# First query block of a fused attention and GEGLU kernel: four key segments, one scheduled step at a time, loads in two waves, output sums preloaded before the last PV

## Chip, cores, metric

The kernel runs on one core of a Trainium2 chip. The metric is the device time of one execution in microseconds (us), and quoted medians are over the executions of a run. All inputs and the output are bf16.

A run is called *fast* or *slow* by its own group: an execution over 1.5% above the fastest of the same kernel is slow.

## The reference, cut to what matters

```python
xn = layernorm(x)                                   # x: 2048 x 448
q, k, v = split(xn @ wqkv)                          # 16 heads of 28
a = softmax(q @ k.T * 28**-0.5) @ v                 # 16 heads, 2048 x 2048 scores
h = gelu_tanh(xn @ w_gate) * (xn @ w_up)            # 448 -> 1792
out = x + concat(a) @ wo + h @ w_down
```

## The kernel before

The kernel is one static program for five engines. Its order is fixed by a scheduler that runs on the host while the program is built. The scores make 1024 units (query block of 512, head group of 4 heads, key tile of 128, head). Three units form a *slot*: three score matmuls into one PSUM tile `st` of 128x1536, then one exp on ScalarE. The exps `e` are later multiplied with v into the tile `ot`; these matmuls are called *PV*. There are 342 slots. Everything else has to fit between the slots, as *steps* of about four matmuls and one copy out of PSUM: transposes of the normalized input, projections of q, k and v, the MLP, the output products, the softmax normalization. All steps share one PSUM buffer (`aux`, one bank), so a step can start on TensorE only after DVE has copied the step before it out.

The first query block is special, because k and v do not exist yet. It runs in two key segments. The first four key tiles of all four head groups come first, then key tiles 4 to 15 of each head group in turn:

```python
SEG = 4
blocks = [(0, hg, 0, SEG) for hg in range(NHG)] + [(0, hg, SEG, NKC) for hg in range(NHG)]
blocks += [(Q, hg, 0, NKC) for Q in range(1, NQ) for hg in range(NHG)]
```

Steps with a deadline (a slot number) stand in `todo`, where `due(Q, hg, kc)` is the slot that first needs key tile `kc` of head group `hg` for query block `Q`; the MLP, the output products and later q projections stand in `lazy`:

```python
for T in range(1, NQ):                      # 512 rows of keys each
    for t0 in (4 * T, 4 * T + 2):
        add(due(0, 0, 4 * T) - 6, 1, lambda t0=t0: g_transpose(t0))
    for hg in range(NHG):
        add(due(0, hg, 4 * T) - 4.5, 1, lambda hg=hg, T=T: g_proj(1, hg, T))
for tt in range(NT):
    add(due(0, 0, tt) + 0.5 if tt >= SEG else 2 + tt, 1, lambda tt=tt: g_v(tt))

def run_slot():
    if cur[0] is None:                      # else: the MLP or output product in hand goes on
        if urgent:                          #       to its last step (up to four slots)
            cur[0] = urgent.pop(0)()
        elif todo and (todo[0][0] <= now[0] + 2 or not lazy):
            cur[0] = todo.pop(0)[2]()
        elif lazy:
            ...
```

In the main loop, a step that has become late is forced into the present slot, and so is the next one. Other steps wait for `credit`, which grows by the steps left over the slots left; a step costs one. `backlog` is the scheduler's estimate of TensorE work still queued, in ns:

```python
if overdue or aux_open[0] or ((credit[0] >= 1.0 or p >= END) and backlog + C_SLOT <= dt + 600):
    ev = run_slot()
    ...                                     # credit -= 1
    while todo and todo[0][0] < p - 0.6:    # still late: a second, a third step in this slot
        ...
        ev = run_slot()
        credit[0] -= 1.0
if not ev and not aux_open[0]:              # no step: dummy matmuls, to keep the clock up
    nj = int((0.85 * dt - backlog) / 216)
    if nj > 0:
        jp = aux.tile([P, QT], F32, tag="a", name="jp")
        junk(jp[:], nj)
        backlog += 216 * nj
```

At the start, the whole q and k weight (784 KB) is loaded before the first head group can be padded into place. At the end, the four output sums so far (`pre`, as a high and a low bf16 part) are put into PSUM by eight identity matmuls behind the last PV:

```python
preload(0)
while len(pv_q) > 4: emit_pv(pv_q.pop(0))
preload(1); preload(2)
while pv_q: emit_pv(pv_q.pop(0))
fb = spool.tile(...); fins[3] = fb[:, 0:D]
preload(3)
otb = ...; nc.scalar.copy(otb[:], ot_cur[0][:])
junk(fa[:, 2 * QT :], 1)
...                                         # sums, reciprocal, product `on`, last output matmuls
```

The softmax here doesn't subtract the row's maximum and nothing guards it: scores larger than these inputs give would overflow.

## Time and profile before

| before | us | from |
|---|---|---|
| median | 565.5 (3 runs, 563.6 to 569.5) | first times |
| profiled execution | span 563.5, clock 0.962 | cores view |
| first exp starts / last exp ends | 15.6 / 552.5 | ScalarE timeline |
| after the last exp | 11.0 | the same |
| 342 exps, 28 tanhs in an unbroken row | about 482 | pitches 1.335 and 0.945 us, estimate |
| idle ScalarE between first and last exp | 55.3 | see below |

The page first: its span, engine totals, and two rows of 40 slices (14.1 us each). Digits are tenths of busy time; PEclk is the granted clock of TensorE in tenths.

```profile
span 563.5 us, 8188 instructions
...
PE 482.1 (86%) x3228; PEld 155.0 (28%) x3253; DVE 256.5 (46%) x491; ACT 501.5 (89%) x383; POOL 13.2 (2%) x44
...
ACT  4679779878669999999998999999999999999993
...
PEclk9699998997679999999999999999999999999999
```

ScalarE (ACT) is the busiest engine, and after slice 13 it is near 9 throughout. Before that it is not, and some low digits stand above a low clock. A table of windows makes two stretches of it: busy time per engine, instruction counts in brackets, then the granted clock.

```profile
core 0: us, PE busy (x) PEld busy (x) DVE busy (x) ACT busy (x) POOL busy (x), PEclk, DMA share, GB/s
0.00:80.00 80.00, 63.87 (x411) 23.22 (x413) 46.13 (x123) 58.31 (x48) 13.18 (x44) 0.94 0.32 75
80.00:190.00 110.00, 91.03 (x552) 26.46 (x558) 46.05 (x80) 89.38 (x67) 0.00 (x0) 0.86 0.10 26
```

Between 80 and 190 us ScalarE is busy for 89.4 of 110 us. For finer numbers I took each exp's and tanh's start in the trace, less the start before it and its pitch (1.335 us after an exp, 0.945 after a tanh); what is left is idle ScalarE. By slot it is 15.1 us in slots 0 to 39, **23.0 us in slots 40 to 99**, and 17.2 us in the 242 slots after. These three numbers are used for every run below; each comes from the one profiled execution of that kernel.

One stall inside, from the timeline (start, duration, engine, line, operation, output from inputs; in brackets how long the engine sat idle before it, and what released it):

```profile
121.02 0.69 DVE L376 TENSOR_TENSOR gu<-gups,g 128x512 bf16<-128x512 f32 x1 [1.19 <-PE gups L326]
121.76 0.38 PE L398 MATMUL bt<-rr_175,sel 128*128 128x512 bf16 x1 [0.78 <-DVE gu L376]
...
122.18 0.69 DVE L401 TENSOR_TENSOR on<-otsb,bt 128x512 bf16<-128x512 f32 x1 [0.47 <-PE bt L398]
122.92 1.02 PE L281 MATMUL pp<-xnT_199,wqk_sb 112*128 112x512 bf16 x4 [0.78 <-DVE on L401]
...
123.98 0.69 DVE L288 CAST kT_3_1428<-pp 128x512 bf16<-128x512 f32 x1 [1.11 <-PE pp L281]
...
124.73 1.02 PE L494 MATMUL st<-qT,kT_3_1428 28*128 28x512 bf16 x6 [0.79 <-DVE kT_3_1428 L288]
...
125.43 1.45 ACT L508 ACTIVATE e<-st 128x1536 bf16<-128x1536 f32 x1 [3.73 <-PE st L494]
```

Three steps (an MLP step, a normalization, a key projection; this is slot 61) pass through the one `aux` buffer one after another, TensorE and DVE taking turns; the scores need the projected key, and ScalarE waits 3.7 us. The window of 3.41 us around it is the last before the clock was halved, and so with another at 87 us (TensorE alone; columns: window, its length, busy time, granted clock):

```profile
87.23:90.65 3.42, 1.38 (x17) 1.00 0.04 7
121.37:124.78 3.41, 1.45 (x9) 1.00 0.23 67
```

The half-clock stretches are 19.0 to 29.2, 90.7 to 94.1, 124.8 to 135.0 and 145.3 to 162.3 us, 41 us together. Last, the tail (timeline; the exps are merged, x2):

```profile
550.44 2.02 ACT L508 ACTIVATE e<-st 128x1536 bf16<-128x1536 f32 x2
...
553.14 0.40 PE L521 MATMUL ot<-e,va_163 128*32 128x512 bf16 x4
553.62 0.59 ACT L786 CAST otb<-ot 128x512 bf16<-128x512 f32 x1 [1.16 <-PE ot L521]
...
554.35 0.35 PE L773 MATMUL f_5956<-prehi,ident 128*128 128x448 bf16 x1
...
555.67 0.35 PE L773 MATMUL fb<-prelo,ident 128*128 128x448 bf16 x1
...
556.07 0.24 PE L789 MATMUL fb<-selc,otb 128*128 128x4 bf16 x4
...
557.63 0.69 DVE L811 TENSOR_TENSOR on<-otb,fb 128x512 bf16<-128x512 bf16 x1 [0.56 <-PE fb L802]
...
560.69 0.35 ACTq L825 DMA_DIRECT2D out_dram<-res  x1
```

The copy `otb` is done at 554.2, but the sums that read it start at 556.07, because the preloads stand in between.

### The profile page before, as it was taken

The numbers are of one execution on the slowest core, as the hardware profiler recorded it, in microseconds if no ns is written. First come the engines' busy times: TensorE is split into PE (matmuls) and PEld (weight loads), VectorE is DVE, ScalarE is ACT, GpSimd is POOL, SyncE is SP. The second block draws the span as 40 slices with busy tenths as digits, with TensorE's granted clock in tenths as the row PEclk, the third lists the DMA queues.
The fourth block names the chain that finished last, engine by engine and source line by source line (L and its number), as shares of the span: only waits on it lengthen the run. The fifth ranks groups of instructions, "written<-read, shape, count | busy, mean of one in ns | idle before, by whom it ended". The sixth has DMA issues, their size and how long they took to land.

```text
span 563.5 us, 8188 instructions
## 1 busy us (share of the span) xinstructions
PE 482.1 (86%) x3228; PEld 155.0 (28%) x3253; DVE 256.5 (46%) x491; ACT 501.5 (89%) x383; POOL 13.2 (2%) x44
## 2 busy tenths in 40 slices
PE   7878788878788888988988899888888898989986
PEld 3223332222222222322222332222222232223322
DVE  5668332443345541155655312666646512671241
ACT  4679779878669999999998999999999999999993
POOL 4310000000000000000000000000000000000000
PEclk9699998997679999999999999999999999999999
DMA  9800000110111100021211002031101101200000
GB/s 212 202 11 1 2 0 2 31 36 1 34 33 28 42 1 18 16 68 33 67 34 34 1 18 58 26 84 49 51 17 34 35 18 49 66 2 0 3 1 33
DMA packets 39685, 20.43 MB, mean 36 GB/s; under 512 B 7328, under 2 KB 39648, under 8 KB 39648
## 3 DMA queue, kind: packets, MB, share of 16 engines
q1 hardware_dynamic: 38560, 18.83, 12.8%
q10 hardware_dynamic: 1088, 1.09, 0.7%
q8 instruction: 25, 0.41, 0.3%
q14 instruction: 12, 0.10, 0.1%
HBM read 17.89 MB, written 1.84 MB: 35 GB/s over the span
## 4 chain that ended last, share of the span: by engine, by line
PE 54%; DVE 18%; ACT 17%; issue 8%; DMA 2%; POOL 0%; ACTq 0%; POOLq 0%; DVEq 0%
PE gups L326 18%; ACT e L508 16%; PE st L494 9%; PE ot L521 9%; PE jp L549 5%; PE op L418 5%; DVE gu L376 4%; PE pp L281 4%; DVE g L337 4%; PE pv L295 3%; DMA wst<-in_A_wqkv_dram 2%; ACT th L357 1%; DVE qT L288 1%; DVE zz L352 1%; DVE on L401 1%
## 5 line engine op out<-in xcount | busy, mean ns | idle before, releaser
L508 ACT ACTIVATE e<-st 128x1536 bf16<-128x1536 f32 x342 | 470.9, 1467 | 44.5 <-PE st L494 38.0
L337 DVE CAST g<-gups 128x512 bf16<-128x512 f32 x56 | 38.7, 691 | 65.6 <-PE gups L326 65.6
L549 PE MATMUL jp<-zt 128*128 128x512 bf16 x124 | 42.9, 396 | 18.5 <-DVE g L337 4.8
L376 DVE TENSOR_TENSOR gu<-gups,g 128x512 bf16<-128x512 f32 x56 | 38.7, 691 | 43.9 <-PE gups L326 43.9
L418 PE MATMUL op<-wd_sb,ht 128*128 128x448 bf16 x224 | 50.7, 354 | 0.8 <-DVE qT L288 0.5
L326 PEld LDWEIGHTS <-wu 112*128 112x128 bf16 x224 | 19.1, 98 | 41.3 <-issue 27.9
L357 ACT ACTIVATE th<-zz 128x1024 bf16<-128x1024 bf16 x28 | 29.9, 1069 | 0.0
L326 PEld LDWEIGHTS <-wg 112*128 112x128 bf16 x224 | 19.0, 98 | 39.3 <-issue 26.6
L549 PEld LDWEIGHTS <-zt 128*128 128x128 bf16 x182 | 16.8, 101 | 36.8 <-issue 28.7
L418 PEld LDWEIGHTS <-ht 128*128 128x128 bf16 x224 | 18.2, 98 | 27.0 <-issue 15.3
L352 DVE TENSOR_TENSOR zz<-po,g 128x1024 bf16<-128x1024 bf16 x28 | 19.2, 687 | 0.5
L368 DVE TENSOR_TENSOR ht<-ph,gu 128x1024 bf16<-128x1024 bf16 x28 | 19.2, 686 | 0.4
L342 DVE TENSOR_TENSOR sq<-g 128x1024 bf16<-128x1024 bf16 x28 | 19.2, 686 | 0.3
L281 PEld LDWEIGHTS <-wqk_sb 112*128 112x128 bf16 x128 | 11.3, 101 | 26.5 <-issue 17.6
L326 PE MATMUL gups<-xnT_199,wu 112*128 112x512 bf16 x56 | 14.4, 379 | 3.7 <-DVE g L337 2.8
L288 DVE CAST qT<-pp 128x512 bf16<-128x512 f32 x15 | 10.4, 691 | 15.4 <-PE pp L281 15.4
L326 PE MATMUL gups<-xnT_199,wg 112*128 112x512 bf16 x56 | 14.4, 380 | 2.5 <-DVE gu L376 1.4
L326 PE MATMUL gups<-xnT_197,wu 112*128 112x512 bf16 x56 | 14.5, 380 | 2.3 <-DVE gu L376 1.8
L326 PE MATMUL gups<-xnT_198,wu 112*128 112x512 bf16 x56 | 14.5, 380 | 2.3 <-DVE g L337 1.4
L326 PE MATMUL gups<-xnT_198,wg 112*128 112x512 bf16 x56 | 14.4, 380 | 2.3 <-DVE g L337 1.8
L326 PE MATMUL gups<-xnT_197,wg 112*128 112x512 bf16 x56 | 14.5, 381 | 1.4 <-DVE g L337 1.4
L418 PE MATMUL op<-wo_sb,on 128*128 128x448 bf16 x60 | 14.1, 354 | 1.3 <-DVE pre L464 1.0
(263 smaller groups left out, 606.4 us busy)
## 6 DMA issues: line engine op xcount, KB each, us to landing
wg<-in_B_w_gate_dram SPq DMA_DIRECT2D x28, 224.0 KB
wu<-in_B_w_up_dram SPq DMA_DIRECT2D x28, 224.0 KB
wd_sb<-in_B_w_down_dram SPq DMA_DIRECT2D x1, 1568.0 KB
out_dram<-res SPq DMA_DIRECT2D x14, 112.0 KB
den<-otsb SPq DMA_DIRECT2D x60, 2.0 KB
rr_174<-recb SPq DMA_DIRECT2D x32, 1.0 KB
x_119<-in_A_x_dram SPq DMA_DIRECT2D x1, 448.0 KB
x_120<-in_A_x_dram SPq DMA_DIRECT2D x1, 448.0 KB
```

Of the source, the lines that this page charges most:

```text
L281: nc.tensor.matmul(pp[:, 0:QT] if ps is None else pp, lhsT=wqk_sb[:, comp, hg, c, :], rhs=xnc(T, c), start=(c == 0), stop=(c == NDC - 1),)
L326: nc.tensor.matmul(ps[:], lhsT=w[:, c, k * P : (k + 1) * P], rhs=xnc(Q, c), start=(c == 0), stop=(c == NDC - 1),)
L337: yield ("evac", C_EVAC, lambda ps=ps, k=k: nc.vector.tensor_copy(g[:, k, :], ps[:]))
L342: nc.vector.tensor_mul(st["a"][:], g[:], g[:])
L352: nc.vector.tensor_mul(st["z"][:], st["b"][:], g[:])
L357: nc.scalar.activation(st["t"][:], st["z"][:], AF.Tanh, scale=TANH_SCALE)
L376: yield ("evac", C_EVAC, lambda ps=ps, k=k: nc.vector.tensor_mul(gu[:, k, :], ps[:], g[:, k, :]))
L418: nc.tensor.matmul(ps[:, 0:D], lhsT=l, rhs=r, start=(first and n == 0), stop=(last and n == len(seq) - 1))
L494: nc.tensor.matmul(st[:, j * QT : (j + 1) * QT], lhsT=kT[(hg, kc // 4)][32 * hh : 32 * hh + Dh, (kc % 4) * P : (kc % 4 + 1) * P], rhs=qT[( ...
L508: nc.scalar.activation(e[:, 0:n], st[:, 0:n], AF.Exp, scale=SCALE)
L521: nc.tensor.matmul(ot_cur[0][32 * hh : 32 * hh + 32, :], lhsT=vaug[kc][:, h * 32 : (h + 1) * 32], rhs=e[:, j * QT : (j + 1) * QT], start=( ...
L549: nc.tensor.matmul(ps, lhsT=zt[:, 0:P], rhs=zt[:], start=True, stop=True)
```

## The change

The intent: spread what the first query block needs, so that no pile forms; start earlier; end earlier.

```diff
-    blocks = [(0, hg, 0, SEG) for hg in range(NHG)] + [(0, hg, SEG, NKC) for hg in range(NHG)]
+    blocks = [(0, hg, k, k + SEG) for k in range(0, NKC, SEG) for hg in range(NHG)]
@@ closing a block: one accumulator per head group, added to in place
@@ layer norm in four groups (statistics from slot 0, 12, 30 on), not two
@@ deadlines
-            add(due(0, 0, 4 * T) - 6, 1, lambda t0=t0: g_transpose(t0))
-            add(due(0, hg, 4 * T) - 4.5, 1, lambda hg=hg, T=T: g_proj(1, hg, T))
-        add(due(0, 0, tt) + 0.5 if tt >= SEG else 2 + tt, 1, lambda tt=tt: g_v(tt))
+            add(first - 6 + k, ln_p0[T] + 10 + 2 * k, lambda t0=4 * T + 2 * k: g_transpose(t0))
+            add(due(0, hg, 4 * T) - 4, ln_p0[T] + 13, lambda hg=hg, T=T: g_proj(1, hg, T))
+            add(first - 2 + 1.4 * k, ln_p0[T] + 13, lambda tt=4 * T + k: g_v(tt))
@@ slot rule: the MLP may be interrupted after each step; eight slots of look-ahead
+        if todo and todo[0][0] <= p + 1:
+            return step(todo.pop(0)[2]())
+        if urgent:
+            return step(urgent.pop(0)())
+        if todo and todo[0][0] <= p + LOOK and todo[0][1] <= p:
+            return step(todo.pop(0)[2]())
+        ...                                   # due q projections, then the MLP in hand, then lazy
-        overdue = bool(urgent) or (todo and todo[0][0] <= p) or (lazy and any(...))
+        overdue = (todo and todo[0][0] <= p) or any(...)
@@ fewer dummies
-            nj = int((0.85 * dt - backlog) / 216)
+            nj = int((0.75 * dt - backlog) / 216) if p < NP - 2 else 0
@@ first wave of loads: x rows 0-511 and the weights of head group 0 alone (196 KB)
+    nc.sync.dma_start(wst0[:, :, 0, :], wv_ap[:, :, 0 : 4 * Dh])
+    nc.scalar.dma_start(wst0[:, :, 1, :], wv_ap[:, :, D : D + 4 * Dh])
+    ...                                       # the rest once these have landed
@@ tail
-    fins = [f0[:, 0:D], fa[:, 0:D], fa[:, QT : QT + D], None]
+    fins = [f0[:, 0:D]] + [fa[:, k * QT : k * QT + D] for k in range(3)]
+    for tl in range(TPQ):
+        preload(tl)
     while pv_q:
         emit_pv(pv_q.pop(0))
-    junk(fa[:, 2 * QT :], 1)                  # and two more places
+    junk(fb[:, 0:QT], 1)
```

No exp, tanh, projection or output product is added or removed. Eight more blocks are closed.

## The prediction

> **What bounds the kernel now.** ScalarE: the page has it busy 89% of 563.5 us. In the timeline, exps in an unbroken row come 1.335 us apart (the last 18 span 23.65 us); a tanh takes about 0.945 us of the row. 342 exps and 28 tanhs need about 482 us (estimate from those pitches). The span is 15.6 us before the first exp, 537 between first and last (482 of work, 55 idle), 11.0 after the last.
>
> Counting exps in slices of the ScalarE timeline, about 38 us of the idle fall before 190 us (81 exps have started by 160 us; an unbroken row would allow 108), 17 us in the 362 us after. The first query block needs all keys and values between slots 21 and 37, then 9 more key projections just ahead of use; its MLP, which could fill TensorE, starts near 100 us. The waits name scores (`st`) and `ot`. At 121-125 us a just-in-time chain shows: bt, DVE, pp, DVE, scores; ScalarE idles 3.7 us. After such gaps the table of windows shows a granted clock of 0.50: about 19-29, 91-94, 125-135 and 145-162 us, 41 us in all; four projection matmuls there take 1.9 us, not 1.0. The Trainium skill, "TensorE: Matmul & The Clock Gate", Part 1, says that an idle TensorE is gated to half clock until busy for a window; the trace agrees.
>
> **What the change does.**
> 1. Four key segments: deadlines fall at slots 21, 42 and 64, and the MLP fills between. No exp, tanh or projection is removed. Added: 8 block closings (0.69 us DVE each; `ot` has one buffer, so TensorE waits up to 0.8 us each); perhaps 2-4 us of it shows.
> 2. One step at a time by deadline, looking 8 slots ahead: fewer chains, fewer cold clocks. The MLP starts early, so later phases thin out.
> 3. Small first load: the chain now waits for the 785 KB `wst`, landing at 10.3 us. The first wave is 200 KB, so pads move to about 8.4 us, after the exp table load; transposes end near 10.1. First exp at about 14 us: gain 1.5-2.
> 4. Tail: 8 preloads (1.5 us) and junk stand between the last exp (552.5) and the sums (556.1). Gain about 2 us; last exp to end about 9.
> 5. Less junk (0.75 for 0.85): some risk of a cold clock.
>
> **Critical path.** Items 1 and 2 hit ScalarE's idle before 190 us. Estimate: 38 falls to about 12 there, 17 to about 14 after. 14 + 482 + 26 + 9 = 531 us span; the measured time was 2 above the span, so **533 us**, range **522 to 547**. Faster by over 2%: 0.94; within 2%: 0.05; slower: 0.01.
>
> **What would show each step.** Right: first exp at 13.5-14.5 us; about 100 exps and tanhs by 160 us; tanhs from about 25-35 us on; clock row near 9 except perhaps one dip in the first 30 us, under 15 us cold; about 9 us after the last exp; counts and pitches unchanged. Wrong: cold stretches of 10 us past 40 us; ScalarE waiting for `st` in slots 21-85; `ot` waits of 1 us at each closing.
>
> **What would make it wrong.** The pile moves to segment boundaries, where transposes, projections and values still chain over one auxiliary PSUM buffer and DVE; MLP weights land late behind the second wave; less junk lets the clock drop in steady state; the MLP competes and the steady 17 us grow. Upside: even load takes steady idle below 10 us: about 522.

## The result and the profile after

The median fell from 564.5 us (4 runs, 558.3 to 569.5) to 536.4 us (4 runs, 536.4 to 538.2). The ratio of the fast runs is 0.9545, with a 95% interval from 0.946 to 0.963. A ratio is the mean time of one kernel's fast runs over that of the other's in the same rounds, so it is not quite the ratio of the quoted medians. The profiled executions took 565.7 us (before, slow) and 538.2 us (after, fast, the slowest of its four); the mean of the fast runs before is 562.4 us, so about 3 us of the difference between the two profiles belong to the slower state.

The same rows of the page after (a slice is now 13.4 us):

```profile
span 536.4 us, 8127 instructions
...
PE 460.5 (86%) x3174; PEld 152.1 (28%) x3194; DVE 265.8 (50%) x514; ACT 498.5 (93%) x382; POOL 18.4 (3%) x71
...
ACT  4777899999999999999999999999999999999993
...
PEclk9686999999999999999999999999999999999999
```

The table of windows:

```profile
0.00:80.00 80.00, 67.09 (x407) 22.90 (x409) 45.36 (x128) 59.85 (x48) 17.80 (x68) 0.85 0.29 78
80.00:190.00 110.00, 93.40 (x669) 30.61 (x671) 63.95 (x115) 107.75 (x83) 0.62 (x4) 1.00 0.10 27
```

Between 80 and 190 us ScalarE is now busy for 107.8 of 110 us. Before 80 us almost nothing has changed: 59.9 us against 58.3, and the clock there is even lower than before.

The whole 27.1 us of span between the two profiled executions can be added up: the first exp comes 1.75 us earlier (13.82 for 15.57), ScalarE's idle falls by 25.0 us (55.3 to 30.3), and the time after the last exp by 0.35 us (11.05 to 10.7). By slot the idle fell by 0.8 us in slots 0 to 39 (to 14.3), by **20.9 us in slots 40 to 99 (to 2.1)** and by 3.3 us after (to 13.9).

Three windows of 3.41 us ahead of the clock drops that remain (TensorE alone):

```profile
13.41:16.82 3.41, 2.07 (x16) 1.00 1.16 304
33.89:37.30 3.41, 1.44 (x18) 1.00 0.00 0
47.54:50.95 3.41, 1.94 (x16) 1.00 0.00 0
```

The clock was halved right after each: 16.8 to 27.1, 37.3 to 47.5 and 51.0 to 54.4 us, 24 us together for 41 before. The middle one in the timeline:

```profile
33.74 0.40 PE L500 MATMUL st<-qT,kT_0_505 28*128 28x512 bf16 x4 [0.46 <-DVE qT L294]
35.71 0.39 PE L500 MATMUL st<-qT,kT_0_505 28*128 28x512 bf16 x3 [1.57 <-ACT e L514]
...
37.39 1.03 PE L287 MATMUL pp<-xnT_201,wqk_sb 112*128 112x512 bf16 x2
```

By its matmul records TensorE waits 1.57 us for an exp, in slots where the scheduler placed no step and a single dummy, because its backlog count said that TensorE was late. That dummy is missing among the matmuls: the program places 88 dummies in the loop, all weight loads are in the trace (this one at 34.06 us), but only 70 of the matmuls. In e6, with the same loop and all 88 records, the window at this place (34.55 to 37.96 us) is busy for 1.76 us with no gap over 1.25 us, and the clock was halved after it too. Two projection matmuls then take 1.03 us; at full clock two took 0.60 (at 15.64 us).

The first tanh comes late, on ScalarE's timeline:

```profile
94.74 1.20 ACT L363 ACTIVATE th<-zz 128x1024 bf16<-128x1024 bf16 x1
```

It was at 114 us before; the MLP still does not fill the first 80 us. The tail:

```profile
523.54 2.17 ACT L514 ACTIVATE e<-st 128x1536 bf16<-128x1536 f32 x2
...
525.31 0.36 PE L777 MATMUL f_5930<-prehi,ident 128*128 128x448 bf16 x1
...
526.93 0.40 PE L527 MATMUL ot<-e,va_159 128*32 128x512 bf16 x4
...
528.05 0.25 PE L788 MATMUL fb<-selc,otb 128*128 128x4 bf16 x4 [0.72 <-ACT otb L785]
...
530.05 0.69 DVE L810 TENSOR_TENSOR on<-otb,fb 128x512 bf16<-128x512 bf16 x1 [0.99 <-PE fb L552]
...
531.76 0.53 ACT L823 CAST res<-fa 128x448 bf16<-128x448 f32 x1 [3.77 <-PE fa L812]
...
532.33 0.62 DVE L823 CAST res<-fa 128x448 bf16<-128x448 f32 x1 [0.51 <-ACT res L823]
532.99 0.53 ACT L823 CAST res<-fa 128x448 bf16<-128x448 f32 x1 [0.69 <-DVE res L823]
```

From the end of the last exp to the sums is 2.3 us (525.71 to 528.05), against 3.6 before (552.46 to 556.07): 1.3 us gained. But the last PV now waits behind the eight preloads (526.93, although its exp ended at 525.71), `on` waits for dummies in its own tile `fb` (0.99 us idle for 0.56 before), and the copies on ScalarE and DVE take turns on tile `fa`, where before one of them read `fb` at the same time. Most of the 1.3 us is given back.

### The profile page after: what moved, and what is told of

Read it like the earlier page. It is cut to its first block, busy times and chain, and to the rows that moved or that the text cites. A ratio compares the mean times of both kernels' runs of the same rounds, so it can differ in the third digit from the quotient of the medians.

```text
span 536.4 us, 8127 instructions
## 1 busy us (share of the span) xinstructions
PE 460.5 (86%) x3174; PEld 152.1 (28%) x3194; DVE 265.8 (50%) x514; ACT 498.5 (93%) x382; POOL 18.4 (3%) x71
## 3 DMA queue, kind: packets, MB, share of 16 engines
q1 hardware_dynamic: 39648, 19.68, 13.3%
HBM read 18.09 MB, written 1.84 MB: 37 GB/s over the span
## 4 chain that ended last, share of the span: by engine, by line
PE 45%; ACT 25%; DVE 15%; issue 13%; DMA 0%; SPq 0%; ACTq 0%; DVEq 0%
ACT e L514 23%; PE gups L332 14%; PE st L500 7%; PE ot L527 7%; PE pp L287 5%; PE op L424 4%; DVE gu L382 3%; DVE g L343 3%; PE jp L552 2%; PE pv L301 2%; ACT th L363 2%; PE jt L552 2%; DVE qT L294 1%; DVE zz L358 1%; DVE otsb L542 1%
## 5 line engine op out<-in xcount | busy, mean ns | idle before, releaser
L552 PE MATMUL jp<-zt 128*128 128x512 bf16 x70 | 23.6, 380 | 10.0 <-DVE gu L382 4.1
L552 PEld LDWEIGHTS <-zt 128*128 128x128 bf16 x123 | 11.5, 102 | 24.8 <-issue 19.0
L542 DVE COPY otsb<-ot 128x512 f32<-128x512 f32 x15 | 10.4, 692 | 16.5 <-PE ot L527 16.5
L332 PE MATMUL gups<-xnT_200,wg 112*128 112x512 bf16 x56 | 14.4, 379 | 3.3 <-DVE g L343 2.8
L332 PE MATMUL gups<-xnT_198,wu 112*128 112x512 bf16 x56 | 14.4, 380 | 3.2 <-DVE g L343 1.4
L332 PE MATMUL gups<-xnT_199,wg 112*128 112x512 bf16 x56 | 14.4, 380 | 2.8 <-DVE gu L382 1.2
L332 PE MATMUL gups<-xnT_198,wg 112*128 112x512 bf16 x56 | 14.4, 380 | 2.4 <-DVE gu L382 1.4
L332 PE MATMUL gups<-xnT_200,wu 112*128 112x512 bf16 x56 | 14.4, 380 | 2.4 <-DVE g L343 0.9
L332 PE MATMUL gups<-xnT_199,wu 112*128 112x512 bf16 x56 | 14.4, 380 | 1.8 <-DVE g L343 1.3
```

The costliest lines, as they stand in the source:

```text
L332: nc.tensor.matmul(ps[:], lhsT=w[:, c, k * P : (k + 1) * P], rhs=xnc(Q, c), start=(c == 0), stop=(c == NDC - 1),)
L552: nc.tensor.matmul(ps, lhsT=zt[:, 0:P], rhs=zt[:], start=True, stop=True)
```

## The experiments

Twelve kernels ran, all with correct results (the labels skip e9, e10 and e12; no such run is on record). Two theories of the main gain stood against each other: the four segments did it (A), or the scheduler did it (B). B was sharpened to D: what cost the time is steps that the scheduler forces two or three into one slot. How often that happens was counted by printing from the scheduler while each program is built; it is a property of the program, not of a run.

The ratios are to runs of the kernel before in the same rounds, whose median was 561.8 to 565.1 us.

| kernel | forced extra steps (in slots) | idle us, slots 0-39 / 40-99 / rest | median us | ratio to before (95%) |
|---|---|---|---|---|
| before | 4 (27, 61, 61, 71) | 15.1 / 23.0 / 17.2 | 564.5 | 1 |
| after | 0 | 14.3 / 2.1 / 13.9 | 536.4 | 0.9545 (0.946 to 0.963) |
| e1 two segments | 3 (23, 28, 29) | 22.0 / 2.9 / 14.4 | 547.0 | 0.972 (0.965 to 0.980) |
| e2 four segments alone | 6 (23, 37, 37, 55, 66, 66) | 11.7 / 24.6 / 17.4 | 564.9 | 1.005 (0.997 to 1.013) |
| e13 old slot rule | 0 | 17.3 / 4.4 / 13.3 | 539.2 | 0.966 (0.957 to 0.976) |
| e14 old deadlines | 0 | 9.1 / 2.3 / 15.3 | 532.9 | 0.953 (0.944 to 0.962) |
| e15 both old | 6 (as e2) | 14.2 / 20.4 / 13.8 | 556.0 | 0.994 (0.983 to 1.004) |

### Which part of the schedule

**e1_two_segments.** The changed kernel with the old segments:

```diff
-    blocks = [(0, hg, k, k + SEG) for k in range(0, NKC, SEG) for hg in range(NHG)]
+    blocks = [(0, hg, 0, SEG) for hg in range(NHG)] + [(0, hg, SEG, NKC) for hg in range(NHG)]
-    ln_p0 = {1: 0, 2: 12, 3: 30}
+    ln_p0 = {1: 0, 2: 8, 3: 13}
```

A first build read half of a product before it was written, because an MLP interrupted between its last steps could be overtaken by its own tanh. The guard that cures it (a tanh waits until both halves are written) leaves the changed kernel's instructions as they were.

> The changed kernel with the first query block back in two key segments (4 and 12 key tiles) and the layer-norm groups moved earlier to suit; the new slot scheduler, first loads and tail stay. A guard makes each tanh wait for both halves of its gu product; in the changed kernel itself that guard alters no instruction. Theory A (the four segments are what removed ScalarE's idle between 80 and 190 us): that idle comes back to about 20 us, span about 555. Theory B (the scheduler that runs one step at a time removed it): that idle stays at about 4 to 8 us, and only the stretch before 80 us may grow by a few us, since 28 steps are again due between slots 21 and 38; span about 537 to 543.

Measured: 547.0 us (545.2 to 548.5). The idle of slots 40 to 99 stays away (2.9 us), and windows show ScalarE busy for 107.4 of 110 us between 80 and 190. So theory A is wrong about where the gain came from. But the early stretch costs more than B allowed: 22.0 us of idle in slots 0 to 39, against 14.3. The keys and values of all rows are due there again, and three forced steps are back with them: 6.9 us of idle stand at slots 26, 31 and 32, three slots after the forced ones. The segments are worth about 10 us with this scheduler, part of it by the same cause.

**e2_four_segments_alone.** The kernel before with the four segments (the same line of `blocks`, and the closing that adds in place):

```diff
-        k = ap0 + ((t - 4) // 2 if t < 8 else 3 + (t - 8))
+        k = ap0 + (t - 4) // 2 if t < 8 else due(0, 0, 4 * (t // 4)) - 12 + t % 4
```

> The kernel before with the four segments (and the closing that adds in place) alone; late layer-norm applies spread so that their buffers come free; old scheduler, loads and tail. Theory A (segments): ScalarE's idle between 80 and 190 us falls from 24 to about 5 us, span about 543. Theory B (scheduler): forced steps still come two or three in one slot once the MLP runs, the half-clock stretches past 90 us stay, span about 555 to 565.

Measured: 564.9 us, ratio 1.005. Nothing is gained. The window of e2, against 89.38 us busy in the kernel before:

```profile
80.00:190.00 110.00, 90.81 (x568) 28.36 (x565) 53.19 (x94) 88.38 (x67) 0.00 (x0) 0.86 0.08 20
```

This also answers a doubt: the profiled execution of before carries a slow label, but the idle between 80 and 190 us stands in this fast one just the same.

**e13_old_slot_rule and e14_old_deadlines.** The changed kernel with the old `run_slot` and overdue rule, and the changed kernel with the old deadlines:

```diff
# e13: run_slot and `overdue` as in the kernel before, deadlines as in the changed one
# e14:
-            add(first - 6 + k, ln_p0[T] + 10 + 2 * k, ...)
+            add(first - 6, ln_p0[T] + 10 + 2 * k, ...)
-            add(due(0, hg, 4 * T) - 4, ...)
+            add(due(0, hg, 4 * T) - 4.5, ...)
-            add(first - 2 + 1.4 * k, ...)
+            add(due(0, 0, 4 * T + k) + 0.5, ...)
```

> The changed kernel with the old slot rule (an MLP step sequence runs to its end before a due step; look-ahead two slots), but with the new deadlines. A count of the program's own schedule gives no forced extra step here, as in the changed kernel; the kernel before has 4, the segments alone 6. Theory D (what cost the kernel before its 24 us between 80 and 190 us is steps forced two or three into one slot, with the half clock that follows): idle in slots 40 to 100 stays under 5 us, span 534 to 541. Rival (interruptible MLP and look-ahead are needed in themselves): 548 or more.

> The changed kernel with the old deadlines (both transposes at once, values half a slot after their first use) and the new slot rule: again no forced extra step. Theory D: under 5 us of idle in slots 40 to 100, span 534 to 541. Rival (the spacing of the deadlines is what matters): 548 or more.

Measured: 539.2 us (538.0 to 542.8) and 532.9 us (530.1 to 534.6). Both are inside D's expectation or just below it (e14), and the idle of slots 40 to 99 is 4.4 and 2.3 us. Neither part is needed by itself, in a kernel that keeps the rest of the change. The spaced deadlines seem even to cost a little, but e14's interval overlaps that of the changed kernel, and its executions had a clock of 0.984 to 0.999 for 0.977 to 0.980.

**e15_old_rule_and_deadlines.** Both edits together.

> The changed kernel with both the old slot rule and the old deadlines; segments, loads, tail and layer-norm plan stay. The count gives 6 forced extra steps, in slots 23, 37, 55 and 66. Theory D: idle in slots 20 to 100 grows from 7 to 25 us or more, most of it after slots 37, 55 and 66, with half-clock stretches past 60 us; span 552 to 563. Rival (layer-norm plan or loads made the gain): it stays at 536 to 541.

Measured: 556.0 us (553.3 to 561.9). The six forced steps are back, and with them 20.4 us of idle in slots 40 to 99 (24.6 us in slots 20 to 99, for 25 expected), and half-clock stretches at 91.5, 118.8 and 149.5 us. The window, to be compared with 107.75 us busy in the changed kernel:

```profile
80.00:190.00 110.00, 91.08 (x585) 29.05 (x583) 55.56 (x100) 92.69 (x69) 1.75 (x9) 0.88 0.08 22
```

The idle can be followed slot by slot. In the traces of before, e1, e2 and e15, ScalarE loses 1.7 to 3.9 us three slots after every one of the 14 slots with a forced step (the scores of slot n + 3 are issued just behind the steps of slot n): before, for example, 3.9 us at slot 64 after slot 61 and 2.9 us at slot 74 after slot 71, followed by 6.1 us at slots 77 to 81 with the clock halved. Not every loss follows a forced step: before also loses 2.8 us at slot 32. After, e13 and e14, with no forced step, lose no more than 1.3 us at any slot from 20 to 99.

So the main gain is shown: it is the removal of late steps forced into one slot. Either of two edits removes them, spaced deadlines or the interruptible rule with look-ahead; with neither, the other parts of the change are worth little.

### The clock

The 22 executions of the kernel before that had run by then show how the clock and the time go together: 554.4 us at a clock of 0.997, 557.6 at 0.982, 561.8 at 0.973, 565.5 at 0.964, 567.5 at 0.957. The program is the same each time. So up to 13 us of this kernel go along with how its thin stretches happen to fall. The Trainium skill, "TensorE: Matmul & The Clock Gate", Part 1, describes a free-running window of 3413 ns over which TensorE's activity is judged, and, with one core at work, a clock that is either full or half. The traces agree: the recorded clock is 1.0 or 0.5 only, the half-clock stretches last 3.41 us or a multiple of it (6.83, 10.24, 17.07, once 20.48), and they start at window edges that differ from run to run.

**e11_before_with_dummies.** Is the clock the whole loss of the kernel before?

```diff
     emit_s(0)
     emit_s(1)
+    junk(jt[:], 6)
             nj = int((0.85 * dt - backlog) / 216)
-            if nj > 0:
+            more = max(nj, 3) if p < 100 else nj
+            if more > 0:
                 jp = aux.tile([P, QT], F32, tag="a", name="jp")
-                junk(jp[:], nj)
-                backlog += 216 * nj
+                junk(jp[:], more)
+                backlog += 216 * max(nj, 0)
```

> The kernel before with uncounted dummy matmuls after the first two score groups and at least 3 in each of the first 100 slots that runs no step; order of all other work unchanged. Of 22 executions of the kernel before so far the fastest, at 554.4 us, had a granted clock of 0.997, while those at 0.957 to 0.966 took 563 to 567. Theory E (clock is only the smaller part of the loss before 190 us): even with the clock kept near 1.0 the span is 552 to 556 and most of the idle before 190 us, 25 us or more, stays. Rival (the clock is the whole loss): 540 or less.

Measured: 561.1 us (558.6 to 562.1) at clocks of 0.992 to 0.999, ratio 1.0035. The number was missed: 552 to 556 was expected. The rival is refuted. Of the 38.1 us of idle before 190 us, 32.6 us stay, as theory E had it. With the clock at 0.98 in the window, ScalarE is not busy for 16 of the 110 us (21 in the kernel before):

```profile
80.00:190.00 110.00, 96.28 (x629) 29.40 (x626) 47.93 (x84) 94.19 (x70) 0.00 (x0) 0.98 0.10 26
```

So most of the loss is the chain itself. Why the dummies gave nothing, while executions that kept the clock without them took 554 us, is open; it may be that dummies in the `aux` buffer delay the steps behind them.

**e4_junk_in_early_gaps.** The changed kernel with dummies in its first 24 slots:

```diff
     emit_s(1)
+    junk(jt[:], 6)
             nj = int((0.75 * dt - backlog) / 216) if p < NP - 2 else 0
+            if p < 24:
+                nj = max(nj, 3)
```

> The changed kernel with 6 dummy matmuls after the first two score groups and at least 3 in each of the first 24 slots that runs no step. Theory C (the idle left before 80 us is mostly TensorE at half clock after thin windows): the three half-clock stretches before 55 us shrink to at most one, the idle before 80 us falls from 14 to about 7 us, span about 529. Rival (the idle is the chain of projections over one auxiliary buffer and DVE, the clock only follows): cold time shrinks but the idle stays within 2 us of 14, span 534 to 538.

Measured: 538.0 us (536.6 to 540.1); no half clock at all in the profiled execution, idle 8.3 us in slots 0 to 39 as theory C had it, but 16.6 us after slot 100 for 13.9. The experiment had a fault: the added dummies were counted in the scheduler's backlog, which moved later steps by whole slots. In 190 of 514 places DVE works on something else than in the changed kernel (names compared without buffer numbers). It says nothing about C either way.

**e5_junk_uncounted.** The same dummies, not counted; the order of DVE's and ScalarE's work is that of the changed kernel:

```diff
+            more = max(nj, 3) if p < 24 else nj
-                junk(jp[:], nj)
-                backlog += 216 * nj
+                junk(jp[:], more)
+                backlog += 216 * max(nj, 0)
```

> The dummy matmuls of the first junk run again, but not counted in the scheduler's backlog, so that the order of all other work stays that of the changed kernel (in the first junk run the count moved later steps by whole slots). Theory C: with the clock kept full before 55 us, the idle before 80 us is about 8 to 9 us, as it was, and the idle after 80 us stays at the changed kernel's 16 us; last exp about 5 to 6 us earlier, span about 531. Rival (what is gained early is always given back later, for instance because TensorE is limited in another way): idle after 80 us grows to about 20 us again and the span stays at 534 to 536.

Measured: 532.5 us (532.2 to 533.6), ratio 0.9516. Idle is 8.1 / 2.2 / 14.0 us: 6 us gained early, nothing given back. C holds. The medians differ by 3.9 us only, because the changed kernel's profiled execution was 1.8 us above its median; the ratios of the two, from different rounds, overlap. The clock row of its page:

```profile
PEclk9999999999999999999999999999999999999999
```

**e8_no_dummy_in_loop.** The changed kernel without the main loop's dummies; they are still counted, so the order stays:

```diff
-            if nj > 0:
-                jp = aux.tile([P, QT], F32, tag="a", name="jp")
-                junk(jp[:], nj)
-                backlog += 216 * nj
+            backlog += 216 * max(nj, 0)
```

> The changed kernel without the dummy matmuls of the main loop; their backlog is still counted, so the order of all other work stays. In the changed kernel's trace 70 dummies make about 15 us of TensorE's 500, and the clock fell only after windows of 3.4 us with TensorE busy 0.61 or less, while the thinnest later windows were at 0.70. If that is the rule of this trace, no window falls below it and the clock stays full after 55 us: span within 2 us of the changed kernel. Rival (the dummies are what keeps the clock): new half-clock stretches past 60 us and 5 us or more lost.

Measured: 541.4 us (538.0 to 550.4). Three of its seven executions are slow (548.0 to 550.4), the four fast ones took 538.0 to 541.4. All seven have a lower clock, 0.925 to 0.959, than any of the changed kernel's. In time the fast runs hardly decide: three of the four lie within about 2 us, as expected. By the clock my expectation fell: the dummies do keep it. Two of its figures were misread as well: the program places 88 dummies, not 70 (18 matmul records are missing from that trace), and the thinnest later window of the changed kernel was not 0.70 busy but 0.64 (2.17 of 3.41 us at 71.4 us, with no drop after it). In the profiled execution (a slow one) new half-clock stretches start at 101.2 and 258.3 us. The windows ahead of them:

```profile
97.83:101.24 3.41, 2.04 (x25) 1.00 0.23 67
254.84:258.25 3.41, 2.02 (x15) 1.00 0.31 86
```

TensorE was busy for 0.60 and 0.59 of these windows; another at 0.59 (from 132.0 us) was passed over. In the fast runs the loss is 1.6 to 5 us; a larger loss is seen in slow ones only.

### Head and tail

**e3_old_head_and_tail.** The changed kernel with the loads, head order and tail of the kernel before.

```diff
-    nc.sync.dma_start(wst0[:, :, 0, :], wv_ap[:, :, 0 : 4 * Dh])      # and its partner
+    nc.sync.dma_start(wst[:, 0:2, :], wv_ap[:, 0:2, 0 : 2 * D])       # 784 KB in two halves, at once
 ... tail, store order and dummies in it as in the kernel before
```

> The changed kernel with the first loads, head order and tail of the kernel before. If head and tail count just what the two traces show (first exp 1.75 us later, end 0.35 us longer), the span grows by about 2 us to 538.5. If the small first load also helps what follows (rival), the idle before 80 us grows as well and the span by 4 us or more.

Measured: 538.1 us (533.1 to 543.1) at clocks of 0.971 to 0.995. The spread of the clock is larger than the 2 us sought, so the time settles nothing. The trace does in part: the first exp starts at 16.1 us for 13.8, and from the last exp's end to the end of the span is 10.6 us with the old tail, for 10.7 with the new one. By the trace the head is worth about 2 us, the tail as changed nothing. The rival is not settled: idle before 80 us is 15.8 us for 14.3, but in an execution labelled slow.

**e6_tail_reordered.** The changed kernel with two of four sums ahead of the last PV, dummies in a bank of their own, and the fourth output back in `fb`:

```diff
-    for tl in range(TPQ):
-        preload(tl)
+    for tl in range(2):
+        preload(tl)
     while pv_q: emit_pv(pv_q.pop(0))
+    fins[3] = fb[:, 0:D]
+    preload(2); preload(3)
     otb = ...
-    junk(fb[:, 0:QT], 1)
-    junk(fb[:, 0:QT], 2)                       # twice
+    junk(jt2[:], 2)                            # twice, a new tile in the bank of `ot`
-        (2, nc.scalar.copy, nc.sync), (1, nc.vector.tensor_copy, nc.sync), (3, nc.scalar.copy, nc.scalar),
+        (1, nc.scalar.copy, nc.sync), (3, nc.vector.tensor_copy, nc.sync), (2, nc.scalar.copy, nc.scalar),
```

> The changed kernel with only two of the four output sums preloaded ahead of the last PV, dummies sent to a bank of their own, and the fourth output back in another tile. Theory: the tail's expected gain went into three new waits (eight preloads 1.2 us ahead of the last PV, a product waiting 0.4 us for dummies in its tile, copies on ScalarE and DVE taking turns on one tile). Last exp's end to span end falls from 10.7 to about 8.7 us, span about 534.5. Rival (these waits hide behind the output DMA): it stays above 10.2 us.

Measured: from the last exp's end to the end 8.9 us, as expected. The time, 535.3 us (530.9 to 537.3), is 1.1 us below the changed kernel's and hidden by the clock's spread (0.972 to 0.992).

**e7_both.** e5 and e6 together.

> Both of the former together. If they add: about 529 us. If the tail's gain is hidden: about 531.

Measured: 530.5 us (530.4 to 531.9), ratio 0.9485 (0.944 to 0.953), the fastest version; 2.0 us below e5 of the same rounds. The trace has both gains whole (8.1 us of idle in slots 0 to 39, 8.9 us after the last exp), so they add, although 530.5 us lies nearer to the 531 expected for a hidden tail than to 529. Its tail:

```profile
521.51 0.40 PE L527 MATMUL ot<-e,va 128*32 128x512 bf16 x4
...
522.63 0.25 PE L793 MATMUL fb<-selc,otb 128*128 128x4 bf16 x4
...
524.20 0.69 DVE L815 TENSOR_TENSOR on<-otb,fb 128x512 bf16<-128x512 bf16 x1 [0.56 <-PE fb L806]
...
525.72 0.97 ACT L828 CAST res<-fa 128x448 bf16<-128x448 f32 x2 [3.15 <-PE fa L817]
525.91 0.62 DVE L828 CAST res<-fb 128x448 bf16<-128x448 f32 x1
```

The last exp ended at 521.05. The last PV follows 0.5 us later (1.2 in the changed kernel), `on` waits 0.56 us as before the change (0.99), and ScalarE and DVE copy at the same time, from two tiles. The waits named in the changed kernel's tail were real and could be taken away; e6 removes all three at once, so what each is worth is read from the traces alone.

## Why the prediction was right or wrong

- **Time.** 533 us with 522 to 547 was predicted, 536.4 measured. The sum of four terms, predicted 14 + 482 + 26 + 9, measured in the profiled execution (538.2 us) 13.8 + 482 + 30.3 + 10.7 (the 482 by the pitches). The sum came out although the MLP did not fill the first segments, as the points below show; to that extent the number was luck.
- **What bounds.** Right: ScalarE's work did not change, and nearly the whole gain is ScalarE's idle before 190 us, 38.1 us before (14.2 by 80 us and 23.9 from there to 190) and 18.2 after.
- **How: the chain and the late steps.** The chain at 121 us was the right witness, but the prediction credited "items 1 and 2" together. Item 1 alone (e2) gives nothing; either spaced deadlines (which the prediction named only as the result of the segments) or the slot rule of item 2 is enough (e13, e14), and without both the loss is back (e15). Going back to two segments costs about 10 us (e1), but there three steps are forced again, so this too is in part the forced steps.
- **"the MLP fills between" and "tanhs from about 25-35 us on".** Wrong. The first tanh came at 94.7 us. Each due step costs one credit, and credit grows by about 0.75 a slot (240 steps of all kinds over 322 slots). In the first 42 slots 29 due steps use it up, and the MLP's first step comes in slot 42, near 85 us. That was in the kernel's code and could have been worked out. The count of exps and tanhs begun by 160 us was right all the same: 99, for about 100.
- **"38 falls to about 12 there".** Too good: 18.2 us, of which 14.3 lie before 80 us. This is the term that was missed most. The runs show why: three half-clock stretches in the first 55 us. With dummies in the gaps (e5) the early idle falls by 6 us.
- **"clock row near 9 except perhaps one dip ..., under 15 us cold".** Wrong: 24 us in three stretches. 41 us fell to 24, not to one dip.
- **First exp at 13.5 to 14.5 us.** Right: 13.8, and e3 undoes it.
- **"Gain about 2 us; last exp to end about 9".** Wrong: 10.7 us. The preloads did move ahead of the sums, but three new waits took most of it back. Without them the tail is 8.9 us (e6, e7).
- **"Less junk: some risk of a cold clock".** No loss seen after 55 us in the changed kernel, at 0.75. Taking all of it away does lower the clock (e8).
- **Eight more closings, 2 to 4 us.** Not seen as such: slots 40 to 99, in which about half of the first block's sixteen closings fall, have 2.1 us of idle in all.

What stays open: whether the slot rule or the spaced deadlines would be enough in the kernel before without the rest of the change (no run has that); why dummies in the kernel before gave it the clock but no time (e11); how the remaining 14 us of idle after slot 100 arise; and the exact rule by which a thin window halves the clock.

## What to carry to other kernels

When steps with deadlines share one buffer, look for slots in which the scheduler forces two or three of them: each is a serial chain that starves the engine you feed, and a count at build time finds them before any run. Spacing the deadlines or letting due work interrupt long work both cure it; finer blocking alone does not. When you move work out of a tail, check what now stands ahead of the last producer, and which copies share a tile; and when you add dummies, keep them out of the cost model, or you test another schedule.

## What the Trainium skill lacked or had wrong

- "TensorE: Matmul & The Clock Gate", Part 1, says that the clock is halved "after ≥1 idle window (~3.4µs)", and the page's closing table advises against gaps of TensorE over about 3 us. Here windows that were 0.40 to 0.61 busy were enough (1.38, 1.45, 1.94, 2.02, 2.04 and 2.07 of 3.41 us), with no gap over 0.8 us in the window at 121.4 us. A passage of Part 1 on PSUM queues does say that frequent short idle times between groups of matmuls make the clock swing, but the page has no figure for how busy a window must be. These runs give no sharp one either: drops also follow windows of 0.65 (e7, 2.22 us at 281.8) and 0.67 (e15, 2.27 us at 211.0), while windows of 0.54 pass without one (e2, 1.84 us at 134.8; e15, 1.85 us at 81.3). The ends of matmul records are modelled, and some records are missing.
- The same part says that one busy window brings the full clock back. In these traces the last half-clock window was busy for 0.90 to 1.00 (the changed kernel: 1.00 in all three), but windows of 0.93 to 0.98, and in the changed kernel one of 1.00 (3.42 us, from 40.7 us), were followed by another at half clock, so stretches of 10.24 and 17.07 us occur in work that never stops for long.
- "PSUM — Partial Sum Buffer", on bank collisions, asks for guarding by bank and quadrant. The three output banks of one tile were copied by ScalarE and DVE strictly in turn (531.76, 532.33, 532.99 us, each released by the other by the profile); with one of them in another tile the copies overlapped (525.72 and 525.91). No page says that a program's waits may go by tile, not by bank.
